# A two-layer product with Mish: x loaded by column quadrants and transposed by VectorE in place of TensorE and DMA transposes

## The chip, the cores and the metric

The kernel runs on one core of a Trainium2 chip. The core has a matrix engine (TensorE, PE in the profile; its weight loads are the row PEld), a vector engine (VectorE, DVE), a scalar engine (ScalarE, ACT), GpSimd (POOL) and SyncE (SP), which here only issues transfers. Transfers (DMAs) are issued from the queues of SP and ACT and carried out by 16 DMA engines. SBUF is the working memory with 128 partitions; PSUM holds the results of the matrix engine in eight banks. The metric is the device time in microseconds; lower is better.

## What is computed

```python
B, S, D, F = 1, 2048, 512, 1792
def reference(x, w1, b1, w2):
    h = jnp.einsum("bsd,df->bsf", x, w1) + b1
    sp = jnp.log1p(jnp.exp(-jnp.abs(h))) + jnp.where(h > 0, h, jnp.zeros_like(h))
    act = h * jnp.tanh(sp)
    return jnp.einsum("bsf,fd->bsd", act, w2)
```

All inputs and the output are bf16. x is 2 MB, w1 and w2 are 1.8 MB each, the output is 2 MB. The activation is Mish.

## The kernel before

The 2048 rows of x are cut into four blocks of 512 rows (16 tiles of 128 rows). For each block a first product makes h transposed: for each of 14 slices f of 128 columns of w1, four matmuls (k = 0 to 3, 128 values of the contraction index each) accumulate in one PSUM bank, 128 x 512; `mish` then reads the bank on ScalarE, adds the bias and writes bf16 to `a_sb` (L159). A second product makes the output tile by tile: for each tile i of 128 rows, 14 matmuls (L198) accumulate over f; VectorE copies the bank to `o_sb` (L204) and SP stores it. Each of the two products has 56 matmuls of 512 columns in a block.

The first product needs x transposed, with the contraction index on the partitions: `xT[:, k, rows]`. Before, this is made in two ways. The first 256 rows are loaded as they lie (`x_nat`, two rows to a partition) and transposed by eight matmuls against an identity (`transpose_x`, L145), four PSUM banks being copied to `xT` by VectorE and ScalarE (L150). The identity is made by GpSimd (L128) and VectorE (L130). All other rows come through four transposing DMAs issued from SP, the first (256 rows) behind a wait for the third filler matmul, the other three behind w2.

Everything is put in order by hand. Each engine has one instruction stream; `Stream.wait` sets a wait on a semaphore and `mark` counts one up. At the start eight filler matmuls on constants (`WARM`, L105) run into bank 7. SP issues, in this order: x_nat; w1 for k = 1, slices 0 to 7; the transposing load of rows 256 to 511; w1 for k = 3; b1; w1 for slices 8 to 13 (768 KB); w2; three transposing loads. ACT issues w1 for k = 0 and k = 2, slices 0 to 7, after the table of Mish is asked for and after b1's buffer is cleared by VectorE. A DMA that waits holds up those behind it on its queue.

The first stage of block 0 opens eight banks at once (`OPEN`, slices 0 to 7) through `first`, with narrow matmuls: tile 0 alone, then tile 1 for k = 0, then tiles 0 and 1, then tiles 2 and 3 together, then the full 512 for k = 3. That makes 8 matmuls of 128 columns, 44 of 256 and 8 of 512; slices 8 to 13 follow with 24 of 512. `spread_b1` turns the bias with four 32x32 transposes on VectorE (L246) and one copy (L248); every `mish` waits for it. In block 0 the second product uses banks 2, 3, 0, 1; in the others banks 0 to 3, while the first product uses banks 4 to 7. The last tile is cut into three parts (`mm2_last`).

Of the kernel before, what the change touches and what calls it, by code (L numbers as in the profile page):

```python
# [5 lines left out]
P = 128  # L6
SQ = 32
WARM = (512,) * 5 + (256,) * 2 + (128,)
# [24 lines left out]
def bass_standalone__dense_activation_mish__prompt_kernel(  # L33
# [17 lines left out]
    w1v = w1.rearrange("(k p) f -> p k f", p=P)  # L51
# [5 lines left out]
    with ExitStack() as es:  # L57
# [3 lines left out]
        x_nat = sb("x_nat", [P, 2, D], BF)  # L61
# [6 lines left out]
        diff = sb("diff", [P, P], dt.int32)  # L68
        ident = sb("ident", [P, P], BF)
# [11 lines left out]
        pool = Stream(nc.gpsimd, sem("c_pool"))  # L81

        def load(q, dst, src, name, transpose=False):
            s = sem(name)
            (q.eng.dma_start_transpose if transpose else q.eng.dma_start)(dst, src).then_inc(s, 16)
            return (s, 16)

        def load_w1(q, ks, a, b):
            return load(q, w1_sb[:, ks, a * P:b * P], w1v[:, ks, a * P:b * P], "s_w1_%d_%d" % (ks.start, a))

        t_w1, t_w2 = {}, {}

        def load_part(q, k0, k1, a, b):
            t = load_w1(q, slice(k0, k1), a, b)
            for f in range(a, b):
                for k in range(k0, k1):
                    t_w1[k, f] = t  # L100

        t_bz = dve.mark(nc.vector.memset(b1_nat[:, :], 0.0))  # L102
        c_w = nc.const_aps.tensor(1.0, [P, P], BF)
        c_m = nc.const_aps.tensor(1.0, [P, 512], BF)
        t_fill = [pe.mark(nc.tensor.matmul(ps[:, 7, 0:n], c_w, c_m[:, 0:n], start=True, stop=True)) for n in WARM]  # L105

        act.eng.preload_act_table(ACT.Mish)  # L107
        act.wait(t_bz)
        for k in (0, 2):
            load_part(act, k, k + 1, 0, OPEN)  # L110
        t_xn = load(sp, x_nat[:, :, :], x2[0:2 * P, :].rearrange("(p j) d -> p j d", p=P), "s_xn")
        load_part(sp, 1, 2, 0, OPEN)
        sp.wait(t_fill[2])
        t_x23 = load(sp, xT[:, :, 2 * P:4 * P], x2[2 * P:4 * P, :], "s_x23", True)
        load_part(sp, 3, 4, 0, OPEN)
# [6 lines left out]
        t_xT = [None]  # L122
        for s in range(1, len(BLOCKS)):
            lo, hi = starts[s], starts[s + 1]
            t_xT.append(load(sp, xT[:, :, lo:hi], x2[lo:hi, :], "s_xT%d" % s, True))


        t_diff = pool.mark(pool.eng.iota(diff[:, :], pattern=[[1, P]], base=0, channel_multiplier=-1))  # L128
        dve.wait(t_diff)
        t_id = dve.mark(nc.vector.tensor_scalar(ident[:, :], diff[:, :], 0, None, ALU.is_equal))  # L130

        free = [[] for _ in range(8)]
        t_cp = {(j, k): t_x23 for j in (2, 3) for k in range(KT)}
        t_mish = {}

        def transpose_x():

            pe.wait(t_xn, t_id)
            for bank, (eng, js, ks) in enumerate(((dve, (0,), (0,)), (act, (1,), (0,)), (dve, (0, 1), (1,)),
                                                  (act, (0, 1), (2, 3)))):  # L140
                n, m = len(ks), len(js)
                for i, k in enumerate(ks):
                    for h, j in enumerate(js):
                        lo = (i * m + h) * P
                        mm = nc.tensor.matmul(ps[:, bank, lo:lo + P], x_nat[:, j, k * P:(k + 1) * P], ident[:, :],  # L145
                                              start=True, stop=True)
                eng.wait(pe.mark(mm))
# [3 lines left out]
                for k in ks:  # L151
                    for j in js:
                        t_cp[j, k] = t
# [107 lines left out]
        for i in range(N0):  # L261
            mm2(i, 0, D, (i + 2) % 4)
# [37 lines left out]
```

## Time and profile before

| | us |
|---|---|
| median of 3 runs | 104.71 |
| the three runs | 104.32, 104.71, 105.37 |
| span of the profiled execution | 103.96 |
| TensorE busy in it | 101.4 |
| ScalarE busy | 39.5 |
| VectorE busy | 13.2 |

The span is the time from the first to the last instruction of one profiled execution, a little less than the device time. "Busy" for matmuls counts overlapped, pipelined instructions, so a busy TensorE is not one at its peak; how fast it runs is read from the distance between the starts of equal matmuls. The chain of waits is followed back from the last instruction, and its pieces are given as start, length and engine with line. In the timeline a row is start, length, engine, line, operation, and how many equal instructions were merged (x). "SPq" and "ACTq" are the queues' issues of DMAs.

### The profile page before, as it was taken

The numbers are of one execution on the slowest core, as the hardware profiler recorded it, in microseconds if no ns is written. First come the engines' busy times: TensorE is split into PE (matmuls) and PEld (weight loads), VectorE is DVE, ScalarE is ACT, GpSimd is POOL, SyncE is SP. The second block draws the span as 40 slices with busy tenths as digits, with TensorE's granted clock in tenths as the row PEclk, the third lists the DMA queues.
The fourth block names the chain that finished last, engine by engine and source line by source line (L and its number), as shares of the span: only waits on it lengthen the run. The fifth ranks groups of instructions, "written<-read, shape, count | busy, mean of one in ns | idle before, by whom it ended". The sixth has DMA issues, their size and how long they took to land.

```text
span 104.0 us, 1180 instructions
## 1 busy us (share of the span) xinstructions
PE 101.4 (98%) x520; PEld 50.0 (48%) x520; DVE 13.2 (13%) x26; ACT 39.5 (38%) x60; POOL 0.4 (0%) x5
## 2 busy tenths in 40 slices
PE   7999999999999999999999999999999999999993
PEld 2888444444444444444444444444444444444472
DVE  1212000112220000022220000022112000021241
ACT  4300899300027777200007777500005777700000
POOL 1000000000000000000000000000000000000000
PEclk9999999999999999999999999999999999999999
DMA  2999999991101000010111000001111000001111
GB/s 70 367 295 368 359 223 193 199 204 50 50 3 47 0 0 6 0 50 12 39 50 50 0 0 3 0 6 50 50 50 50 0 0 0 0 0 56 52 50 50
DMA packets 12833, 7.94 MB, mean 76 GB/s; under 512 B 7836, under 2 KB 12188, under 8 KB 12828
## 3 DMA queue, kind: packets, MB, share of 16 engines
q1 hardware_dynamic: 12396, 7.33, 26.8%
q10 hardware_dynamic: 432, 0.54, 1.5%
q8 instruction: 4, 0.07, 0.3%
q14 instruction: 1, 0.01, 0.0%
HBM read 3.94 MB, written 2.10 MB: 58 GB/s over the span
## 4 chain that ended last, share of the span: by engine, by line
PE 98%; ACT 0%; issue 0%
PE ps L176 47%; PE ps L198 47%; PE ps L105 3%; PE ps L145 1%; ACT o_sb L228 0%
## 5 line engine op out<-in xcount | busy, mean ns | idle before, releaser
L159 ACT ACTIVATE a_sb<-ps,b_sb 128x512 bf16<-128x512 f32 x56 | 37.1, 698 | 48.5 <-PE ps L176 48.5
L176 PE MATMUL ps<-xT,w_sb 128*128 128x512 bf16 (+2 forms) x252 | 50.0, 361 | 0.0
L198 PE MATMUL ps<-w_sb,a_sb 128*128 128x512 bf16 (+3 forms) x252 | 49.1, 355 | 0.0
L176 PEld LDWEIGHTS ps<-xT,w_sb 128*128 128x128 bf16 x252 | 25.0, 101 | 24.1
L198 PEld LDWEIGHTS ps<-w_sb,a_sb 128*128 128x128 bf16 x252 | 23.2, 98 | 25.6
L204 DVE CAST o_sb<-ps 128x512 bf16<-128x512 f32 x15 | 10.4, 692 | 80.8 <-PE ps L198 80.8
L228 ACT ACTIVATE o_sb<-ps 128x64 bf16<-128x64 f32 x1 | 0.2, 224 | 11.5 <-PE ps L198 11.5
L105 PE MATMUL ps<-const-bfloat16-1.0 128*128 128x512 bf16 (+2 forms) x8 | 2.8, 532 | 0.8 <-PEq L285 0.8
L105 PEld LDWEIGHTS ps<-const-bfloat16-1.0 128*128 128x128 bf16 x8 | 1.0, 136 | 2.2 <-issue 2.1
L150 ACT ACTIVATE xT<-ps 128x128 bf16<-128x128 f32 (+1 forms) x2 | 0.9, 438 | 2.2 <-PE ps L145 2.2
L107 ACT ACT_TABLE_LOAD x1 | 1.3, 1283 | 0.7 <-PEq L285 0.7
L246 DVE STREAM_TRANSPOSE b_T<-b_nat 32x32 bf16<-32x32 bf16 x4 | 0.8, 202 | 3.1 <-DMA b_nat<-in_b_dram 3.0
L145 PE MATMUL ps<-ident,x_nat 128*128 128x128 bf16 x8 | 1.0, 309 | 0.0
L150 DVE CAST xT<-ps 128x128 bf16<-128x128 f32 (+1 forms) x2 | 0.7, 358 | 2.5 <-PE ps L145 2.4
L228 DVE CAST o_sb<-ps 128x320 bf16<-128x320 f32 (+1 forms) x2 | 0.8, 392 | 1.5 <-PE ps L198 1.5
L145 PEld LDWEIGHTS ps<-ident,x_nat 128*128 128x128 bf16 x8 | 0.8, 138 | 0.2 <-DMA x_nat<-in_x_dram 0.2
L130 DVE TENSOR_SCALAR ident<-diff 128x128 bf16<-128x128 int32 x1 | 0.2, 227 | 0.2 <-POOL diff L128 0.2
L128 POOL IOTA diff<- 128x128 int32 x1 | 0.2, 234 | 0.4 <-POOLq L285 0.4
L102 DVE MEMSET b_nat<- 32x64 uint32 x1 | 0.1, 112 | 0.8 <-PEq L285 0.8
L248 DVE CAST b_sb<-b_T 128x14 f32<-128x14 bf16 x1 | 0.2, 176 | 0.0
L285 POOL MEMSET const-bfloat16-1.0<- 128x1 bf16 x1 | 0.1, 101 | 0.0
L285 POOL MEMSET const-uint8-127<- 128x1 uint8 x1 | 0.1, 101 | 0.0
(2 smaller groups left out, 0.2 us busy)
## 6 DMA issues: line engine op xcount, KB each, us to landing
out_dram<-o_sb SPq DMA_DIRECT2D x15, 128.0 KB, 1.7
w_sb<-in_w_dram SPq DMA_DIRECT2D x1, 1792.0 KB, 10.5
w_sb<-in_w_dram SPq DMA_DIRECT2D x1, 768.0 KB, 5.8
w_sb<-in_w_dram ACTq DMA_DIRECT2D x2, 256.0 KB, 3.7
w_sb<-in_w_dram SPq DMA_DIRECT2D x2, 256.0 KB, 3.6
x_nat<-in_x_dram SPq DMA_DIRECT2D x1, 256.0 KB, 2.6
out_dram<-o_sb SPq DMA_DIRECT2D x1, 112.0 KB, 1.7
xT<-in_x_dram SPq DMA_TRANSPOSE x4, 5.2
```

The costliest lines, as they stand in the source:

```text
L105: t_fill = [pe.mark(nc.tensor.matmul(ps[:, 7, 0:n], c_w, c_m[:, 0:n], start=True, stop=True)) for n in WARM]
L107: act.eng.preload_act_table(ACT.Mish)
L128: t_diff = pool.mark(pool.eng.iota(diff[:, :], pattern=[[1, P]], base=0, channel_multiplier=-1))
L130: t_id = dve.mark(nc.vector.tensor_scalar(ident[:, :], diff[:, :], 0, None, ALU.is_equal))
L145: mm = nc.tensor.matmul(ps[:, bank, lo:lo + P], x_nat[:, j, k * P:(k + 1) * P], ident[:, :], start=True, stop=True)
L150: t = eng.mark(nc.vector.tensor_copy(dst, src) if eng is dve else act.eng.activation(dst, src, ACT.Copy))
L159: t = act.mark(act.eng.activation(a_sb[:, f, starts[s]:starts[s + 1]], ps[:, bank, 0:n], ACT.Mish, bias=b1_sb[:, f:f + 1]))
L176: return nc.tensor.matmul(ps[:, bank, lo:hi], w1_sb[:, k, f * P:(f + 1) * P], xT[:, k, starts[s] + lo:starts[s] + hi], start=first, stop=( ...
L198: return nc.tensor.matmul(ps[:, bank, 0:hi - lo], a_sb[:, f, i * P:(i + 1) * P], w2_sb[:, f, lo:hi], start=(f == 0), stop=(f == FT - 1))
L204: t = dve.mark(nc.vector.tensor_copy(o_sb[:, i, lo:hi], ps[:, bank, 0:hi - lo]))
L228: t = eng.mark(nc.vector.tensor_copy(dst, src) if eng is dve else act.eng.activation(dst, src, ACT.Copy))
L246: t = dve.mark(nc.vector.transpose(b1_T[j * SQ:(j + 1) * SQ, :], b1_nat[:, j * SQ:(j + 1) * SQ]))
```

## The change

All of x is now loaded in 256-byte pieces. For each of four column quadrants q (128 of the 512 columns) one DMA brings rows lo to hi to the 32 partitions 32q to 32q + 31 of `x_q`, with row 32j + t of x on partition 32q + t. VectorE then transposes 32x32 blocks, with every fourth column of a quadrant taken together, straight into `xT`. So contraction index 4p + k stands on partition p of `xT[:, k]`, and w1 is read with the same numbering. The matmul transposes, the identity, the transposing DMAs, the GpSimd pattern and the interleaved rows of the first 256 outputs are gone. The filler is five matmuls of 512 and two of 128 columns.

Loads of block 0 come in three lots (tile 0, tile 1, tiles 2 and 3), quadrants 0 and 1 on SP and 2 and 3 on ACT, with w1 in pieces of four slices between them; the rest of x comes on SP behind w2, one DMA for each quadrant, 384 KB. On VectorE the transposes of block 0 stand ahead of the bias; those of block 1 stand behind the first output copy, those of blocks 2 and 3 behind the four output copies of block 0. The first stage now runs tile 0 for slices 0 to 3, tile 1 for slices 0 to 3, tiles 0 and 1 for slices 4 to 7, tiles 2 and 3 slice by slice with the Mish after each, and then slices 8 to 13.

```diff
-WARM = (512,) * 5 + (256,) * 2 + (128,)
+WARM = (512,) * 5 + (128,) * 2
-    w1v = w1.rearrange("(k p) f -> p k f", p=P)
+    w1v = w1.rearrange("(p k) f -> p k f", k=KT)
-        x_nat = sb("x_nat", [P, 2, D], BF)
+        x_q = sb("x_q", [P, S // SQ, P], BF)
+        def load_x(eng, q, lo, hi):
+            src = x2[lo:hi, q * P:(q + 1) * P].rearrange("(j t) c -> t j c", t=SQ)
+            t_x[q, lo] = load(eng, x_q[q * SQ:(q + 1) * SQ, lo // SQ:hi // SQ, :], src, "s_x_%d_%d" % (q, lo))
...
+        load_x(sp, 0, 0, P)
+        load_x(sp, 1, 0, P)
+        load_w1(sp, 0, 1, 0, 4)
+        load_w1(sp, 2, 3, 0, 4)
+        load_x(sp, 0, P, 2 * P)
+        load_x(sp, 1, P, 2 * P)
+        load_w1(sp, 0, 2, 4, OPEN)
+        load_x(sp, 0, 2 * P, 4 * P)
+        load_x(sp, 1, 2 * P, 4 * P)
+
+        load_x(act, 2, 0, P)
+        load_x(act, 3, 0, P)
+        load_w1(act, 1, 2, 0, 4)
         act.eng.preload_act_table(ACT.Mish)
+        load_w1(act, 3, 4, 0, 4)
+        load_x(act, 2, P, 2 * P)
+        load_x(act, 3, P, 2 * P)
+        load_w1(act, 2, 4, 4, OPEN)
+        load_x(act, 2, 2 * P, 4 * P)
+        load_x(act, 3, 2 * P, 4 * P)
         sp.wait(t_bz)
         t_b1 = load(sp, b1_nat[0:FT, :], b1.rearrange("(j p) -> j p", p=P), "s_b1")
-        load_part(sp, 0, KT, OPEN, FT)
+        load_w1(sp, 0, KT, OPEN, FT)
         t = load(sp, w2_sb[:, :, :], w2v, "s_w2")
...
+        for q in range(Q):
+            load_x(sp, q, 4 * P, S)
...
+        def spread_x(lo, hi):
+            frm = max(b for b in (0, P, 2 * P, 4 * P) if b <= lo)
+            dve.wait(*[t_x[q, frm] for q in range(Q)])
+            src = x_q[:, lo // SQ:hi // SQ, :].rearrange("p j (r k) -> p k j r", k=KT)
+            for k in range(KT):
+                dst = xT[:, k, lo:hi].rearrange("p (j t) -> p j t", t=SQ)
+                t = dve.mark(nc.vector.transpose(dst, src[:, k]))
+                for i in range(lo // P, hi // P):
+                    t_xT[i, k] = t
...
-        transpose_x()
+        spread_x(0, P)
+        spread_x(P, 2 * P)
+        spread_x(2 * P, 4 * P)
         t_b1c = spread_b1()
-        first(range(4), (0,), (0,))
-        first(range(4), (1,), (0,))
-        first(range(4, OPEN), (0, 1), (0,))
-        first(range(OPEN), (0, 1), (1, 2))
-        first(range(OPEN), (2, 3), (0, 1, 2))
-        first(range(OPEN), None, (3,), True)
+        first(range(4), (0,))
+        first(range(4), (1,))
+        first(range(4, OPEN), (0, 1))
+        for f in range(OPEN):
+            mm1(0, f, (4 + f) % 8, (2, 3))
         for f in range(OPEN, FT):
             mm1(0, f, (4 + f) % 8)
         for i in range(N0):
             mm2(i, 0, D, (i + 2) % 4)
+            if i == 0:
+                spread_x(starts[1], starts[2])
+        for s in range(2, len(BLOCKS)):
+            spread_x(starts[s], starts[s + 1])
```

More of the change, by code (lines that the diff above doesn't have):

```diff
@@ L134, in bass_standalone__dense_activation_mish__prompt_kernel @@
[L134 to L147, printed above, removed]
-                dst = xT[:, ks[0]:ks[0] + n, js[0] * P:(js[-1] + 1) * P]
-                src = ps[:, bank, 0:n * m * P].rearrange("p (k t) -> p k t", k=n)
-                t = eng.mark(nc.vector.tensor_copy(dst, src) if eng is dve else act.eng.activation(dst, src, ACT.Copy))
-                for k in ks:
-                    for j in js:
-                        t_cp[j, k] = t
-                free[bank] = [t]
+        for q in range(Q):
+            load_x(sp, q, 4 * P, S)
@@ L166, in mm1_step @@
             n = BLOCKS[s]
[L167 removed]
+            js = range(n // P) if js is None else js
+            lo, hi = js[0] * P, (js[-1] + 1) * P
             first = k == 0 and lo == 0
```

71 lines of the change are left out of this document (22 added, 49 removed).

## The prediction

> **What bounds the kernel now.** I read the busy table first, then the chain of waits in order of time, then the timeline of the first microseconds.
>
> ```profile
> span 104.0 us, 1180 instructions
> PE 101.4 (98%) x520; PEld 50.0 (48%) x520; DVE 13.2 (13%) x26; ACT 39.5 (38%) x60; POOL 0.4 (0%) x5
> ...
> PEclk9999999999999999999999999999999999999999
> ```
> ```profile
> 0.73 0.04 issue
> 0.77 2.82 PE ps L105 x8
> 3.60 0.85 PE ps L145 x8
> 4.45 13.01 PE ps L176 x84
> 17.46 12.09 PE ps L198 x56
> 29.55 12.09 PE ps L176 x56
> ...
> 102.15 0.02 issue
> 102.18 0.22 ACT o_sb L228
> ```
>
> The chain is TensorE from 0.77 to 102.15 without a hole: eight filler matmuls (L105), eight transposing matmuls (L145), then the real work. Nothing else ends last until the final copy and store. So the change can only act by when the real work starts, by how fast the array runs then, by the number of matmuls, or by opening a hole. How fast it runs shows in the starts of equal matmuls (first and last start, by line and window):
>
> ```profile
> L145 PE MATMUL ps<-ident,x_nat x8: 296/311/311, 3.4 to 4.1; 128*128 128x128 bf16 x8
> L176 PE MATMUL ps<-xT,w_sb x8: 311/311/311, 4.2 to 5.0; 128*128 128x128 bf16 x8
> L176 PE MATMUL ps<-xT,w_sb x38: 272/273/273, 6.1 to 10.2; 128*128 128x256 bf16 x38
> L198 PE MATMUL ps<-w_sb,a_sb x12: 219/219/219, 100.8 to 101.5; 128*128 128x128 bf16 x12
> ```
>
> A 128-wide matmul takes 0.107 us early (0.85 / 8 in the chain) and about 0.056 late (12 between 100.8 and 101.5); the 38 of 256 take 0.11 each; a 512-wide one 0.216 (12.09 / 56). So TensorE runs at half speed from 0.77 to about 6.1 and at full speed after. The page's clock row reads full throughout; the spacing is the better witness. This halves the worth of any earlier start.
>
> ```profile
> 0.74 0.40 SPq L85 DMA_DIRECT2D x_nat<-in_x_dram  x1
> 0.95 0.86 ACTq L85 DMA_DIRECT2D w_sb<-in_w_dram  x2
> 1.20 0.41 SPq L85 DMA_DIRECT2D w_sb<-in_w_dram  x1
> 3.40 0.78 PEld L145 LDWEIGHTS ps<-ident,x_nat 128*128 128x128 bf16 x8 [0.18 <-DMA x_nat<-in_x_dram]
> 4.25 13.22 PE L176 MATMUL ps<-xT,w_sb 128*128 128x128 bf16 x84
> 4.72 0.95 SPq L85 DMA_DIRECT2D w_sb<-in_w_dram  x2
> 7.48 0.90 DVE L246 STREAM_TRANSPOSE b_T<-b_nat 32x32 bf16<-32x32 bf16 x4 [3.00 <-DMA b_nat<-in_b_dram]
> 10.88 7.63 ACT L159 ACTIVATE a_sb<-ps,b_sb 128x512 bf16<-128x512 f32 x13 [5.79 <-PE ps L176]
> ```
>
> x is there at 3.40, the first real matmul starts at 4.25, right behind the eight transposes.
>
> **The change, part by part.** *Fillers and transposes.* The filler is now five of 512 and two of 128: at half speed 5 x 0.427 (4 x 0.107) + 2 x 0.107 from 0.77 ends at 3.12. The eight transposes (0.85) leave the path, with their four PSUM copies on VectorE and ScalarE, the index pattern on GpSimd and the identity. What replaces them is a wait.
>
> *When tile 0 and its weights are there.* The prices:
>
> ```profile
> x_nat<-in_x_dram SPq DMA_DIRECT2D x1, 256.0 KB, 2.6
> w_sb<-in_w_dram ACTq DMA_DIRECT2D x2, 256.0 KB, 3.7
> w_sb<-in_w_dram SPq DMA_DIRECT2D x1, 768.0 KB, 5.8
> w_sb<-in_w_dram SPq DMA_DIRECT2D x1, 1792.0 KB, 10.5
> ```
> ```profile
> 2.50:3.50 1.00, 1.00 (x7) 0.47 (x5) 0.00 (x0) 0.00 (x0) 0.00 (x0) 1.00 1.05 373
> 19.00:20.00 1.00, 1.00 (x6) 0.48 (x5) 0.00 (x0) 0.08 (x1) 0.00 (x0) 1.00 1.27 289
> ```
>
> An issue takes 0.46 of its queue (0.74 to 1.20 on SP). The transfers run at 373 GB/s with weight rows (first window) and at 289 GB/s with the transposing loads (second), whose pieces of x are the nearest row for the new 256-byte pieces. The 256 KB of x_nat landed 2.6 after issue; at 373 GB/s its data need 0.7, so 1.9 is delay at both ends for a first transfer. Tile 0 comes in four quadrants, two on each queue, issued at 0.74 and 1.20: the second pair lands at 1.20 + 1.9 + 0.2 at the latest, 3.3; if only part of the 1.9 repeats, 2.9. w1's first piece (k = 0, 128 KB) is third on SP, issued at 1.65. Counted in bytes (131 KB of x, then 262 KB for k = 0 and 1, 1.05 at 373) it lands at 0.74 + 1.9 + 1.05 = 3.7; counted from its own issue with the full 1.9 and 0.35 of data, 3.9. I take 3.8 for the first real matmul, with 3.3 and 4.25 as ends. VectorE's part is in front of that:
>
> ```profile
> L246 DVE STREAM_TRANSPOSE b_T<-b_nat 32x32 bf16<-32x32 bf16 x4 | 0.8, 202 | 3.1 <-DMA b_nat<-in_b_dram 3.0
> L204 DVE CAST o_sb<-ps 128x512 bf16<-128x512 f32 x15 | 10.4, 692 | 80.8 <-PE ps L198 80.8
> L150 DVE CAST xT<-ps 128x128 bf16<-128x128 f32 x1 | 0.3, 292 | 2.4 <-PE ps L145 2.4
> ```
>
> A transpose of 32 columns takes 0.20 and a column about 1.04 ns (692 - 292 over 384), so 0.30 for 128 columns, 0.43 for 256, 0.70 for 512. The stride of four elements in the source appears in no row: 0.20 and twice the estimate are the ends, I take the estimate. Tile 0's k = 0 is ready by 3.3 to 3.6, under the weights, and each further k 0.30 later, while TensorE spends 0.43 on the four matmuls of a k.
>
> Weighed against this, the Trainium skill, "SBUF — State Buffer", Door 1, says that a transfer into 32 partitions reaches only 8 of 16 ports and measured 189 GB/s at 1 MiB; by that tile 0's bytes would take about 0.25 longer (an estimate), the start would move to 4.05 and the time by half of it, 0.13. No row here shows a 32-partition load, so the sum keeps 289.
>
> *Worth of the start.* By 6.1 the kernel before has done (6.1 - 4.25) / 2 = 0.93 us of full-speed work; a start at 3.8 has done 1.15. Gain 0.22 (ends: 0.48 and 0).
>
> *More matmuls.* The first stage has 32 of 128, 48 of 256 and 24 of 512 where it had 8, 44 and 32: 20 more for the same columns. Four of 0.056 against one of 0.216 cost 0.008, two of 0.109 cost 0.002: in all 0.05.
>
> *The loads that follow.* The same byte count gives: w1 for k = 2, 3 at 4.4 (needed 4.7); x tile 1 at 4.9 and 5.2 transposed (needed 3.8 + 16 x 0.107 = 5.5); w1 for f 4 to 7 at 6.3 (needed 6.7); x tiles 2 and 3 at 7.2, their k = 0 to 3 transposed at 7.6 to 8.9 (needed 8.4 to 8.8); w1 for f 8 to 13 at 9.3 (needed 11.9); w2, 10.5 from an issue inside 4.72 to 5.67 before and now 0.6 later (twelfth on SP, 0.74 + 11 x 0.46 = 5.8), by 16.3 (needed 17.1). Only tiles 2 and 3 touch, for 0.1 at most: 0 to 0.2 is the bound, I take 0. SP now issues nine loads ahead of b1 and w1's last part, which is in those times; ACT issues nine without its wait for the cleared b1, and its table load follows the third.
>
> *The bias and Mish.* On VectorE the bias now stands behind the transposes of tiles 2 and 3: 8.9 + 1.1 (7.48 to the copy's end) = 10.0; the first Mish waits for it from 8.9. Fourteen Mish at 0.57 (7.63 for 13) end at 18.1; the second product needs the last at 17.1 + 13 x 0.216 = 19.9. Hidden.
>
> *The rest of x.*
>
> ```profile
> 20.52 0.69 DVE L204 CAST o_sb<-ps 128x512 bf16<-128x512 f32 x1 [11.93 <-PE ps L198]
> ```
>
> Four loads, 1.57 MB of 256-byte pieces behind w2: 5.4 at 289 GB/s, landing at about 21 to 22. VectorE reaches their transposes after the first output copy (near 20.5), needs 4 x 0.70, and holds back the next three copies, whose banks nobody needs before the next second product near 41. The first matmul that needs them is near 29.3. Cover: 5 us; without it TensorE would stand by the excess.
>
> **Sum.** -0.22 + 0.05 = -0.17 on a span of 103.96. The median shown, 104.71, stands 0.75 above that span, and the runs spread from 104.32 to 105.37. Forecast 104.5, no change that a measurement can tell (about 1%, 1.05 us, is that bound).
>
> **Rivals.**
> *The clock rises late (slower).* Before, TensorE was busy without a break from 0.77, and full speed came after 5.3 us of it. Now it stands from 3.12 to about 3.8. If this pause makes the count begin again, full speed comes at 3.8 + 5.3 = 9.1 and the work until then loses (9.1 - 6.1) / 2 = 1.5: 106.0. Between 0 and 0.7 us lies the length from which it decides; the trace has no pause to show where. For it: full speed needed long activity. Against: the pause is an eighth of those 5.3 us (0.68 / 5.3). The Trainium skill, "TensorE: Matmul & The Clock Gate", Part 1, gives a free-running window of about 3.4 us that must be busy; by it a missed window costs about 1.7, an estimate. The 5.3 us before agree with up to two such windows. Chance 0.25.
> *The start does not move.* If the weights for k = 0 land at 4.2, as with the two 256 KB loads before (3.7 from issues after 0.95), only the 0.05 is left: 104.8. For it: x's small pieces stand ahead of them on both queues. Against: half the bytes. Chance 0.10.
> *The rest of x is late.* At under 120 GB/s the 1.57 MB take over 13 us and the first product of the second block waits from 29.3; at 100 GB/s by some 3 us: 107.5. Against: 289 GB/s in the trace. Chance 0.03.
> *Everything lands at once.* Work starts at 3.3, and the clock rises as before: 104.71 - 0.48 + 0.05 = 104.3. Chance 0.07.
>
> **How the numbers follow.** The forecast has 0.55; its own range is 104.0 to 105.1. Slower by over 1% (above 105.76): most of the late clock (0.19, since a late start of the full speed falls differently in each run) and the late x, 0.03, and 0.02 of scatter: 0.24. Faster by over 1% (below 103.66) needs the early start and a lucky spread of runs: 0.08. Within: 0.68. The range 103.9 to 106.0 leaves out about 0.1 on each side.
>
> **What would show it.** Chain of waits: no L145, a hole or a wait before the first real matmul between 3.1 and 4.0; 104 matmuls in the first stage, then 12.09 per 56 as before. Starts of 128-wide matmuls going from 0.107 to 0.056 apart near 6.1 (right) or near 9 (late clock). Waits of VectorE on x: tile 0 landed by 3.3; the rest by 22. I am wrong if TensorE shows holes after 5 us, if a 128-column transpose takes over 0.45, or if x's loads run well under 289 GB/s.

## The result and the profile after

| | before | after |
|---|---|---|
| median, us (six runs each) | 104.84 | 109.67 |
| lowest to highest, us | 104.32 to 105.37 | 109.29 to 110.30 |
| span of the profiled execution, us | 103.96 | 108.98 |
| end of the last matmul in it, us | 102.15 | 107.18 |

The ratio of after to before is 1.046, with a 95% interval of 1.0415 to 1.0508: the change costs 4.6%, where no measurable change was forecast. The matmuls end 5.03 us later, and the tail behind them is the same, so the loss is in the array's own row. Here and below, a run more than 1.5% above the fastest of its kernel counts in the medians and not in the ratios. The page of the kernel after:

```profile
span 109.0 us, 1232 instructions
...
PE 103.2 (95%) x522; PEld 51.8 (48%) x531; DVE 22.5 (21%) x47; ACT 38.9 (36%) x58; POOL 0.2 (0%) x4
...
GB/s 43 237 237 238 357 347 218 142 169 147 39 48 48 48 0 6 0 0 48 23 25 48 48 3 0 6 0 48 48 29 19 48 0 0 0 6 48 48 48 48
```

TensorE's share fell from 98% to 95%, and one slice of the GB/s row is 2.72 us: from 2.7 to 10.9 us the loads ran at 237 GB/s. The chain of waits of the kernel after (start, length, what; L173 is the first product, L192 the second; "issue" is time in which nothing that the profile shows was waited for):

```profile
3.53 6.24 DMA w_sb<-in_w_dram
9.77 0.05 issue
9.81 4.46 PE ps L173 x20
...
14.36 3.01 ACT a_sb L160 x5
17.36 5.13 PE ps L173 x23
22.49 5.61 PE ps L192 x26
```

Before, the chain was TensorE from 0.77 on. Now it runs through a load of weights from 3.53 to 9.77, and TensorE's unbroken part begins at 9.81. (From 14.36 to 17.36 the chain follows the Mish; the matmuls start 0.11 apart there, as before and after it, but for 0.32 at 17.04, which leaves room for two matmuls missing from the trace.) The timeline shows what came before:

```profile
0.77 2.50 PE L103 MATMUL ps<-const-bfloat16-1.0 128*128 128x512 bf16 x7 [0.77 <-PEq L274]
...
3.58 0.89 DVE L146 STREAM_TRANSPOSE xT<-x_q 128x128 bf16<-128x128 bf16 x4 [2.67 <-DMA x_q<-in_x_dram]
...
4.92 1.89 PE L173 MATMUL ps<-xT,w_sb 128*128 128x128 bf16 x16 [1.65 <-DMA w_sb<-in_w_dram]
...
7.28 0.89 DVE L146 STREAM_TRANSPOSE xT<-x_q 128x128 bf16<-128x128 bf16 x4 [2.81 <-DMA x_q<-in_x_dram]
...
7.65 1.89 PE L173 MATMUL ps<-xT,w_sb 128*128 128x128 bf16 x16 [0.84 <-DVE xT L146]
...
9.81 10.52 PE L173 MATMUL ps<-xT,w_sb 128*128 128x256 bf16 x61 [0.28 <-DMA w_sb<-in_w_dram]
...
11.66 1.42 DVE L146 STREAM_TRANSPOSE xT<-x_q 128x256 bf16<-128x256 bf16 x4 [3.50 <-DMA x_q<-in_x_dram]
```

Three waits stand where before there was none: for the first weights until 4.92, for tile 1 of x until 7.65, and for w1's slices 4 to 7 until 9.81. The matmuls' durations, by start, show the array's speed. The same view as in the prediction, for two stretches of the kernel after:

```profile
L173 PE MATMUL ps<-xT,w_sb x20: 394/421/422, 9.8 to 13.8; 128*128 128x256 bf16 x20
L173 PE MATMUL ps<-xT,w_sb x28: 272/273/310, 14.1 to 17.0; 128*128 128x256 bf16 x28
```

A 256-wide matmul is recorded with 421 ns and starts 0.21 after the last one until 14.1, then with 273 ns and 0.11: full speed came at 14.1, against 6.1 before. That accounts for the whole loss:

- The first matmul of the product starts 4.92 − 4.25 = 0.67 later. Sixteen of 128 at half speed take 16 × 0.107 = 1.71, so the first lot is issued by 6.63 and TensorE stands 1.02 until 7.65; the second lot is issued by 9.36, and it stands 0.45 until 9.81. Together 2.14.
- From 4.92 to 14.12, less these 1.47 of standing, 7.73 us of real work ran at half speed, which loses 3.87. Before it was (6.10 − 4.25) / 2 = 0.93. The difference is 2.94.
- 2.14 + 2.94 = 5.08, against 5.03 measured.

The loads in the two stretches, before and then after (the last column is GB/s, the one before it the share of the 16 DMA engines that were busy, which this view can show above 1):

```profile
2.60:6.00 3.40, 3.40 (x26) 2.63 (x24) 0.72 (x2) 0.88 (x2) 0.00 (x0) 1.00 1.11 355
6.00:10.40 4.40, 4.40 (x42) 3.93 (x41) 0.98 (x5) 0.00 (x0) 0.00 (x0) 1.00 1.03 334
```
```profile
2.60:6.00 3.40, 1.75 (x15) 1.23 (x13) 0.89 (x4) 0.83 (x1) 0.00 (x0) 1.00 0.79 212
6.00:10.40 4.40, 3.28 (x27) 2.60 (x26) 0.89 (x4) 0.00 (x0) 0.00 (x0) 1.00 1.02 243
```

In the second stretch the 16 DMA engines are as busy as before (share 1.02 against 1.03) and move 27% less (243 against 334).

### The profile page after: what moved, and what is told of

Same layout as the page of the kernel before. It is cut to its first block, busy times and chain, and to the rows that moved or that the text cites. A ratio compares the mean times of both kernels' runs of the same rounds, so it can differ in the third digit from the quotient of the medians.

```text
span 109.0 us, 1232 instructions
## 1 busy us (share of the span) xinstructions
PE 103.2 (95%) x522; PEld 51.8 (48%) x531; DVE 22.5 (21%) x47; ACT 38.9 (36%) x58; POOL 0.2 (0%) x4
## 4 chain that ended last, share of the span: by engine, by line
PE 86%; DMA 6%; ACT 3%; SPq 2%; issue 1%; ACTq 0%
PE ps L192 44%; PE ps L173 42%; DMA w_sb<-in_w_dram 6%; ACT a_sb L160 3%; SPq L83 2%; ACT o_sb L222 0%; ACTq L26 0%
## 5 line engine op out<-in xcount | busy, mean ns | idle before, releaser
L173 PE MATMUL ps<-xT,w_sb 128*128 128x512 bf16 (+2 forms) x268 | 53.0, 364 | 3.0 <-DMA w_sb<-in_w_dram 1.9
L192 PE MATMUL ps<-w_sb,a_sb 128*128 128x512 bf16 (+3 forms) x247 | 48.8, 355 | 0.3
L173 PEld LDWEIGHTS ps<-xT,w_sb 128*128 128x128 bf16 x272 | 27.7, 107 | 27.5 <-DMA w_sb<-in_w_dram 2.5
L192 PEld LDWEIGHTS ps<-w_sb,a_sb 128*128 128x128 bf16 x252 | 23.2, 98 | 25.6
L146 DVE STREAM_TRANSPOSE xT<-x_q 128x512 bf16<-128x512 bf16 (+2 forms) x24 | 10.5, 500 | 10.5 <-DMA x_q<-in_x_dram 10.5
L222 ACT ACTIVATE o_sb<-ps 128x64 bf16<-128x64 f32 x1 | 0.2, 223 | 11.5 <-PE ps L192 11.5
L103 PE MATMUL ps<-const-bfloat16-1.0 128*128 128x512 bf16 (+1 forms) x7 | 2.5, 534 | 0.8 <-PEq L274 0.8
## 6 DMA issues: line engine op xcount, KB each, us to landing
x_q<-in_x_dram SPq DMA_DIRECT2D x4, 384.0 KB, 10.5
```

Of the source, the lines that this page charges most:

```text
L146: t = dve.mark(nc.vector.transpose(dst, src[:, k]))
L173: return nc.tensor.matmul(ps[:, bank, lo:hi], w1_sb[:, k, f * P:(f + 1) * P], xT[:, k, starts[s] + lo:starts[s] + hi], start=first, stop=( ...
L192: return nc.tensor.matmul(ps[:, bank, 0:hi - lo], a_sb[:, f, i * P:(i + 1) * P], w2_sb[:, f, lo:hi], start=(f == 0), stop=(f == FT - 1))
L222: t = eng.mark(nc.vector.tensor_copy(dst, src) if eng is dve else act.eng.activation(dst, src, ACT.Copy))
```

## The experiments

Two causes were possible after this reading, and they feed each other: loads that come late, and a clock that rises late because of the holes. A first group tells them apart; a second changes the loads in the changed kernel; a third puts the new parts into the old order. The times are medians; each ratio is to the kernel before, run beside it on the same chip. In the runs with another order of x or of w1's rows, what is multiplied is not the reference's.

| run | what | us | ratio (95%) |
|---|---|---|---|
| e8_pause | before, fewer fillers | 105.96 | 1.011 (1.007 to 1.015) |
| e1_fill | after, fillers in the holes | 109.03 | 1.041 (1.036 to 1.047) |
| e5_w1rows | after, w1 rows as before | 109.79 | 1.043 (1.037 to 1.049) |
| e6_w1wide | after, w1 in wider pieces | 109.95 | 1.047 (1.042 to 1.052) |
| e2_ports | after, x to 128 partitions | 107.98 | 1.031 (1.025 to 1.037) |
| e3_rows1k | after, x in pieces of 1024 bytes | 109.29 | 1.037 (1.025 to 1.049) |
| e4_one | after, x in one load a lot, 128 partitions, 1024 bytes | 108.36 | 1.033 (1.025 to 1.041) |
| e12_one256 | as e4, 256 bytes | 109.59 | 1.048 (1.042 to 1.053) |
| e7_all | e4, e5 and e6 together | 108.31 | 1.027 (1.019 to 1.034) |
| e9_all_fill | e7 with a longer filler | 106.33 | 1.015 (1.010 to 1.020) |
| e10_ports_fill | e2 with fillers | 108.36 | 1.033 (1.029 to 1.038) |
| e11_old_order | old order and plain loads, VectorE transposes | 105.02 | 1.002 (0.999 to 1.004) |
| e13_x_alone | old order, x in quadrants | 108.36 | 1.030 (1.024 to 1.036) |
| e14_q128 | e13, 128 partitions | 107.98 | 1.026 (1.018 to 1.035) |
| e15_r32 | e13, 1024 bytes | 107.95 | 1.024 (1.016 to 1.032) |
| e16_one | e13, one load a lot, 128 partitions, 1024 bytes | 105.65 | 1.006 (1.003 to 1.010) |
| e17_one256 | as e16, 256 bytes | 108.11 | 1.031 (1.026 to 1.036) |

### The clock, and the loads

**e8_pause.** The kernel before, with three fillers in place of eight, so that TensorE stands before its transposes and nothing else is late.

```diff
-WARM = (512,) * 5 + (256,) * 2 + (128,)
+WARM = (512,) * 3
```

> The kernel before with only three filler matmuls (they end near 2.05), so that TensorE stands until x is there at 3.4; nothing else is changed, the first real matmul starts at 4.25 as before. Theory 'late clock': the pause of 1.3 us makes full speed come between 6.8 and 10.2 instead of 4.2 to 7.6, on the mean 2.6 later, half of it lost: time 105.3 to 106.4 against 104.6. Rival 'the clock does not mind': 104.4 to 104.9.

The same view of the first product's matmuls in e8_pause, for two stretches:

```profile
L176 PE MATMUL ps<-xT,w_sb x16: 314/421/421, 4.9 to 8.0; 128*128 128x256 bf16 x15, 128*128 128x128 bf16 x1
L176 PE MATMUL ps<-xT,w_sb x28: 272/273/310, 8.2 to 11.2; 128*128 128x256 bf16 x28
```

A pause of 1.3 us moved full speed from 6.1 to 8.3, and (8.3 − 6.1) / 2 is 1.1; the median rose by 1.0. So a late clock by itself exists, at half of its lateness, as the first rival had it.

**e1_fill.** The changed kernel with fillers in its three holes, so that the clock can rise while the loads stay as they are.

```diff
-WARM = (512,) * 5 + (128,) * 2
+WARM = (512,) * 9 + (128,) * 2
...
+        def fill(n):
+            for _ in range(n):
+                pe.mark(nc.tensor.matmul(ps[:, 3, 0:512], c_w, c_m[:, 0:512], start=True, stop=True))
...
         first(range(4), (0,))
+        fill(4)
         first(range(4), (1,))
+        fill(2)
```

> The changed kernel with TensorE kept busy in its three early holes by matmuls on constants (four of 512 columns more at the start, four between tile 0 and tile 1, two before slices 4 to 7). The loads are untouched. Theory 'late loads': the holes and the half speed both come from data that arrive late, and full speed alone buys little, because tiles 2 and 3 still land at 11.5 us and their transposes end near 13.1: full speed by 6 to 7.5 us, first stage done about 1 us earlier, time 108.4 to 109.0 against 109.67. Rival 'late clock': the 2.9 us lost to half speed are the main cost by themselves: time 106.5 to 107.2.

The timeline of e1_fill (L236 is the filler in the holes):

```profile
7.28 1.05 PE L173 MATMUL ps<-xT,w_sb 128*128 128x128 bf16 x16
...
8.17 0.60 PE L236 MATMUL ps<-const-bfloat16-1.0 128*128 128x512 bf16 x2
...
9.34 1.92 PE L173 MATMUL ps<-xT,w_sb 128*128 128x256 bf16 x16 [0.57 <-DMA w_sb<-in_w_dram]
...
11.01 1.10 DVE L146 STREAM_TRANSPOSE xT<-x_q 128x256 bf16<-128x256 bf16 x3 [3.23 <-DMA x_q<-in_x_dram]
...
11.52 0.61 PE L173 MATMUL ps<-xT,w_sb 128*128 128x256 bf16 x2 [0.26 <-DVE xT L146]
```

Sixteen matmuls now take 1.05 in place of 1.89: the array is at full speed, and was from 3.6. The time gains half a per cent at most (1.041 against 1.046, with intervals that overlap), because TensorE runs into the same loads sooner: slices 4 to 7 at 9.34, tiles 2 and 3 only at 11.5. With these late loads a quick clock is worth little.

### Which loads, in the changed kernel

**e5_w1rows** numbers w1's rows as before, **e6_w1wide** loads slices 0 to 7 of each k at once, as before, in pieces of 2048 bytes in place of 1024.

```diff
-    w1v = w1.rearrange("(p k) f -> p k f", k=KT)
+    w1v = w1.rearrange("(k p) f -> p k f", p=P)
```

> The changed kernel with w1's rows numbered as before (row k * 128 + p on partition p instead of 4p + k); x stays 4p + k, so what is multiplied is not the reference's. Pieces, bytes and order are the same. Theory 'interleaved rows' (every fourth row of w1 is slow to read: single pieces of w1 took 0.4 to 0.9 us in the changed kernel): the weights of slices 4 to 7 land before 8.8 instead of 9.77 and 10.35, long pieces vanish, time 108.5 or less. Rival 'small pieces of x': no change, 109.3 to 110.0.

```diff
-        load_w1(sp, 0, 1, 0, 4)
-        load_w1(sp, 2, 3, 0, 4)
+        load_w1(sp, 0, 1, 0, OPEN)
+        load_w1(sp, 2, 3, 0, OPEN)
...
-        load_w1(sp, 0, 2, 4, OPEN)
...
```

> The changed kernel with w1's slices 0 to 7 in four loads of 256 KB (2048-byte pieces, one for each k, as before) instead of four of 128 KB and two of 256 KB in 1024-byte pieces. The order of the rest stays. Theory 'small pieces of w1': the bytes up to tiles 2 and 3 are the same, and they land by 10.3 instead of 11.54; the first matmul is later by up to 0.5 since k = 0 brings twice the bytes; time 109.0 or less. Rival: the small pieces of x alone set the rate, tiles 2 and 3 land at 11.3 or later, time 109.3 to 110.3.

Neither moved the time beyond its interval, so the form of w1 alone does not make the loss. Its narrower pieces do have a part in the low rate: in e6 the two stretches ran at 278 and 312 GB/s, against 212 and 243, and tiles 2 and 3 landed at 9.44 in place of 11.54. What that gained went to the first matmul, which waited until 5.74 for a load of twice the size. In e5 the two stretches ran at 220 and 265.

**e2_ports, e3_rows1k, e4_one** change x's loads: to all 128 partitions, still in four loads of 256-byte pieces; to 32 partitions in pieces of 1024 bytes; and in one load for a lot, 128 partitions, 1024 bytes. x's values then lie in another order.

```diff
+            m, b = (hi - lo) // P, lo // SQ
+            src = x2[lo:hi, q * P:(q + 1) * P].rearrange("(j p) c -> p j c", p=P)
+            t_x[q, lo] = load(eng, x_q[:, b + q * m:b + (q + 1) * m, :], src, "s_x_%d_%d" % (q, lo))
```

> The changed kernel with x's loads writing all 128 partitions instead of 32: the same number of DMAs, the same 256-byte pieces of the same bytes in the same order, 128 partitions x fewer pieces each. x lies in another arrangement in SBUF, so what is multiplied is not the reference's. Theory 'partitions' (a load into 32 partitions is slow in itself): the rest of x runs at 250 GB/s or more and lands by 25 instead of 27.65, tile 1 lands before 6.2 instead of 7.16, time 107.5 or less. Theory 'pieces' (256-byte pieces) and theory 'count' (many small DMAs): no change, 109.3 to 110.0.

```diff
+            n = (hi - lo) // Q
+            src = x2[lo + q * n:lo + (q + 1) * n, :].rearrange("(n t) d -> t n d", t=SQ)
+            dst = x_q[q * SQ:(q + 1) * SQ, lo // SQ:hi // SQ, :].rearrange("t (n j) c -> t n (j c)", j=Q)
+            t_x[q, lo] = load(eng, dst, src, "s_x_%d_%d" % (q, lo))
```

> The changed kernel with x's loads in 1024-byte pieces (whole rows): the same number of DMAs, still 32 partitions each, the same bytes in all, a quarter of the pieces. x lies in another arrangement in SBUF, so what is multiplied is not the reference's. Theory 'pieces': the early loads and the rest of x gain a rate of 300 GB/s or more, tile 1 lands before 6.2, time 107.5 or less. Theory 'partitions': 32 partitions still bind, no change, 109.3 to 110.0. Theory 'count': the same, no change.

```diff
+            src = x2[lo:hi, :].rearrange("(n p) d -> p n d", p=P)
+            dst = x_q[:, lo // SQ:hi // SQ, :].rearrange("p (n j) c -> p n (j c)", j=Q)
+            t = load(eng, dst, src, "s_x_%d" % lo)
...
-        load_x(sp, 1, 0, P)
...
```

> The changed kernel with one DMA for each lot of x (tile 0 on SP, tile 1 and tiles 2 and 3 on ACT, the rest on SP) in place of four, 128 partitions and 1024-byte pieces. x lies in another arrangement in SBUF, so what is multiplied is not the reference's. All three theories of the loads expect a gain here: tile 1 landed by 5.5, no hole over 0.3 us after the first real matmul, time 104.5 to 106.5. If it stays above 108, the loads of x are not the cause, and the weights' pieces or their row order are. Theory 'count' expects this run alone to gain, the two others near 109.7.

Tiles 2 and 3 landed at 9.71 in e2, 10.42 in e3 and 8.49 in e4, against 11.54, and full speed came at 8.2, 10.5 and 10.1. Each brings the loads forward, none gains half of the loss, and e3's gain is within its interval. The times of e2 and e4 lie in none of the windows that were expected, e3's at the edge of "no change". By what was expected of e4, a time above 108 would clear x's loads; e13 and e16, below, show that this reading would have been wrong: the late clock and w1's narrower pieces were still in it.

**e12_one256** is e4 in pieces of 256 bytes.

```diff
-            src = x2[lo:hi, :].rearrange("(n p) d -> p n d", p=P)
+            src = x2[lo:hi, :].rearrange("(p n) (j c) -> p (n j) c", p=P, j=Q)
...
```

> The run with one DMA for each lot of x (e4_one), but in 256-byte pieces (each quarter row goes to a place of its own with a gap; 128 partitions; four times the pieces). What is multiplied is not the reference's. Against e4_one only the pieces differ; against e2_ports (four DMAs for each lot, 256-byte pieces, 128 partitions) the number of DMAs does. Theory 'count': as in e4_one, all of the first 1.57 MB landed by 8.9 (8.49 there), time 107.7 to 108.8. Theory 'pieces': landed at 9.4 or later, near e2_ports' 9.71.

Tiles 2 and 3 landed at 10.61 in place of e4's 8.49, and what e4 had gained is gone: in one load to 128 partitions the small pieces cost by themselves. The number of loads is not idle either: e2 has the same small pieces and 128 partitions, in four loads over both queues, and is faster than e12 (1.031 against 1.048). Why is not shown.

**e7_all** takes e4, e5 and e6 together; **e9_all_fill** is e7 with ten fillers of 512; **e10_ports_fill** is e2 with e1's fillers before tile 0 and between tiles 0 and 1.

> The changed kernel with all three at once: one DMA for each lot of x (128 partitions, 1024-byte pieces), w1's rows as before, w1's slices 0 to 7 in 2048-byte pieces; VectorE still transposes, the filler stays short. What is multiplied is not the reference's. Theory 'late loads, then late clock': the loads keep 340 GB/s or more from 3 to 9 us, tiles 2 and 3 land by 7.8, only the pause before the first matmul and one before tile 1 are left; time 105.5 to 107.0. If the clock played no part, it would come to 104.6 to 105.4. If it stays above 107.5, something else in the change costs.

```diff
-WARM = (512,) * 5 + (128,) * 2
+WARM = (512,) * 10 + (128,) * 2
```

> The run with one DMA for each lot of x, w1's rows and pieces as before (e7_all), and five filler matmuls of 512 columns more, which end near 5.2, where its first real matmul started (5.1). What is multiplied is not the reference's. Theory 'late loads and late clock together are the whole loss': with neither, the first product of block 0 ends at about 18.1 against 17.3 before (the first matmul is still 0.9 later), time 105.0 to 106.0, some 2.5 under e7_all's 108.31. Rival 'something else in the change costs' (the transposes' order, narrow matmuls, the Mish behind them): it stays above 107.

```diff
-WARM = (512,) * 5 + (128,) * 2
+WARM = (512,) * 9 + (128,) * 2
...
         first(range(4), (0,))
+        fill(4)
```

> The run with x's 256-byte pieces written to 128 partitions (e2_ports) and filler matmuls through its two pauses (four of 512 more at the start, four between tile 0 and tile 1). What is multiplied is not the reference's. Loads as in e2_ports: tile 1 at 6.8, slices 4 to 7 at 8.9, tiles 2 and 3 at 9.7. Theory 'loads bind once the clock is up': tiles 2 and 3 are ready from 10.1 to 11.2, the first product of block 0 ends near 19 to 19.5, time 106.3 to 107.0. If the clock alone were left: 105.0 to 105.8.

The loads of e7 and e9 run at the old rate and more: the stretches 2.6 to 6.0 and 6.0 to 10.4 of e7_all:

```profile
2.60:6.00 3.40, 1.56 (x12) 0.92 (x9) 0.89 (x4) 0.00 (x0) 0.00 (x0) 1.00 1.04 381
6.00:10.40 4.40, 4.29 (x34) 3.70 (x33) 3.18 (x13) 0.00 (x0) 0.00 (x0) 1.00 1.07 372
```

Yet e7 is still 2.7% slower, with full speed only at 11.0; e9, where it comes at 4.8, is 1.5% slower. e7 missed its expectation by 1.3 us, e9 by 0.3. Loads alone take the ratio from 1.046 to 1.027, the clock alone (e1) to 1.041, both to 1.015. That is more than the sum, as if each hid the other, but the intervals are too wide to show the excess. What is left in e9 is in its first stage: the weights for k = 0, second on SP, land at 5.38, so that the first matmul starts at 5.43 in place of 4.25, and those for k = 2 land at 6.34, with TensorE standing until 6.38. e10 missed its expectation by over 1 us, and its fillers gained nothing over e2 (1.033 against 1.031). Its loads of x and w1 are those of e2, but in the profiled execution tiles 2 and 3 landed at 10.67 in place of 9.71 and slices 4 to 7 up to 0.8 later, and TensorE stood 1.20 for the slices: equal loads can differ by about 1 us from one execution to another, and a profile of one execution can't settle differences of that size.

### One part at a time, in the old order

**e11_old_order** keeps the order of the kernel before, its w1 and its bank order, but loads x in plain rows and makes all transposes on VectorE; e11b_old_order is a second execution of it with its own profile. x's columns are numbered 4p + k there and w1's rows are not. The filler is longer than before.

```diff
-WARM = (512,) * 5 + (256,) * 2 + (128,)
+WARM = (512,) * 5 + (256,) * 5 + (128,) * 2
...
-        t_x23 = load(sp, xT[:, :, 2 * P:4 * P], x2[2 * P:4 * P, :], "s_x23", True)
+        t_x23 = load(sp, x_r[:, 2:4, :], x2[2 * P:4 * P, :].rearrange("(n p) d -> p n d", p=P), "s_x23")
...
-        transpose_x()
+        spread(x_nat[:, :, :], t_xn, 0, 2 * P)
+        spread(x_r[:, 2:4, :], t_x23, 2 * P, 4 * P)
```

> The kernel before, its order of matmuls and loads kept, with every transpose moved to VectorE's 32x32 blocks (no identity, no transposing matmuls, no transposing DMAs; all of x in plain loads of whole rows into 128 partitions) and the filler lengthened to about 4.2, where the first weights land. VectorE's blocks land in an arrangement of x that is not the reference's, so what is multiplied is not. Theory 'the transposes on VectorE are free, the loss is in how and in which order the loads come': first real matmul at 4.1 to 4.3, no hole over 0.3 after it, 104.4 to 105.2, the same as before within 0.5. Rival 'VectorE's transposes cost by themselves': 105.8 or more, with TensorE waiting for VectorE.

> e11_old_order once more, for a profile: eleven of its twelve runs took 104.5 to 105.4, but the profiled one 275, with every 512-wide matmul at about 0.6 us to the end. Expected: 104.5 to 105.5, first real matmul at 4.1 to 4.3, no hole after it.

The chain of waits of e11b_old_order (L157 is the first product):

```profile
2.24 4.48 DMA x_r<-in_x_dram
...
6.74 0.46 DVE xT L136
...
7.24 9.70 PE ps L157 x56
16.94 12.09 PE ps L179 x56
```

The ratio is 1.002 (0.999 to 1.004): in place of TensorE's and the transposing DMAs', VectorE's transposes, with the longer filler, cost no time that the runs can tell, and gain none. They are not free on the way: x for tiles 2 and 3 lands at 6.72, VectorE's first transpose of it stands on the chain for 0.46, and TensorE stands 0.5 until 7.24, where no hole over 0.3 was expected. The first product still ends at 16.94, before 17.46 of the kernel before, because in this execution full speed came at 3.5 in place of 6.1, which is worth 0.9. How much of the equal time the filler pays for was not tried apart.

**e13_x_alone** is the kernel before with x loaded and transposed as in the kernel after (four loads a lot, 32 partitions, 256 bytes) and w1's rows numbered to match; w1's pieces, the order of the loads on SP and the order of the matmuls stay; two of the four loads of each lot now go through ACT, the first two of them ahead of w1. The filler runs to 4.6.

```diff
-        t_xn = load(sp, x_nat[:, :, :], x2[0:2 * P, :].rearrange("(p j) d -> p j d", p=P), "s_xn")
+        t_xn = [load_x(eng, q, 0, 2 * P) for q, eng in enumerate((sp, sp, act, act))]
...
-        t_x23 = load(sp, xT[:, :, 2 * P:4 * P], x2[2 * P:4 * P, :], "s_x23", True)
+        t_x23 = [load_x(eng, q, 2 * P, 4 * P) for q, eng in enumerate((sp, sp, act, act))]
```

> The kernel before's order of matmuls, w1's slices 0 to 7 in 2048-byte pieces one k after the other, filler to about 4.6; x comes as in the changed kernel, in column quadrants of 32 partitions and 256-byte pieces (tiles 0 and 1 in one lot), w1's rows as 4p + k, transposes on VectorE. It computes the reference. Against e11_old_order (105.02, the same as before) only x's loads and w1's row numbers differ. Theory 'x's quadrant loads are the cause': first weights later than 5.0, tiles 2 and 3 later than 9, holes after the first matmul, 107 or more. Theory 'w1's narrow pieces and the order that needs four k at once are': 105.0 to 106.0. Between the two if both count.

The chain of waits of e13_x_alone:

```profile
1.71 4.33 DMA w_sb<-in_w_dram
6.05 0.05 issue
6.09 13.93 PE ps L159 x84
20.02 12.09 PE ps L181 x56
```

x itself is early (its first lot landed by 3.6), and what is late is the weights behind it: k = 0 at 6.05 in place of 4.1, and the product starts 1.84 later than before. Part of that is place in the queue: k = 0 is issued at 1.71 where it was 0.95, and k = 1 lands ahead of it, at 5.34. Full speed, which came at 6.1 before, comes at 9.4; with (9.4 − 6.1) / 2 = 1.7 us lost to half speed, against 0.93, the clock adds 0.75. The first product ends at 20.02, 2.56 later, which is the sum of the two. After its start there is no hole, where holes were expected. x's loads, with the late clock that they bring, carry 3.0 of the 4.6% in this order.

**e14_q128, e15_r32, e16_one, e17_one256** take e13's loads of x apart, as e2, e3, e4 and e12 did in the changed kernel; the lines of their loads are those of these four.

> e13_x_alone with one thing changed: each of the four loads of x in a lot goes to all 128 partitions, still in 256-byte pieces (another order of rows and columns, so the output is not the reference's). In e13 the weights for k = 0 landed at 6.05 us and the run took 108.36. Theory 'the 32 partitions': 104.8 to 106.4, weights for k = 0 landed by 4.9. Theory 'the 256-byte pieces': 107.0 or more, weights at 5.5 or later. Theory 'four loads instead of one': also 107.0 or more.

> e13_x_alone with one thing changed: each of the four loads of x in a lot brings whole rows of 1024 bytes, still to 32 partitions (the output is not the reference's). Theory 'the 32 partitions': 107.0 or more, weights for k = 0 landed at 5.5 us or later. Theory 'the 256-byte pieces': 104.8 to 106.4, weights by 4.9. Theory 'four loads instead of one': 107.0 or more.

> e13_x_alone with x in one load for each lot, whole rows of 1024 bytes to all 128 partitions (the output is not the reference's); weights, their numbering, order and filler as in e13. If the form of x's loads is the cause: 104.4 to 105.7, weights for k = 0 landed by 4.4 us, ratio under 1.01. If the numbering of w1's rows or the longer filler carries part of e13's 3%: 106.0 or more.

> e16_one with one thing changed: each load of x (one for a lot, 128 partitions) is cut into pieces of 256 bytes instead of 1024 (the output is not the reference's). In e16 the first lot landed at 4.75 us and the first matmul of the product started at 5.37; 105.65. Theory 'only the count of loads matters (four for a lot instead of one)': 105.2 to 106.2, first lot landed by 5.0. Theory 'the 256-byte pieces cost by themselves too': 106.8 or more, first lot landed at 5.4 or later.

The weights for k = 0 landed at 5.88 in e14 and 6.78 in e15, and the product started near 5.9 and 6.8. The chains of waits of e16_one and, after it, e17_one256:

```profile
0.73 4.02 DMA x_q<-in_x_dram
...
4.78 0.46 DVE xT L139
5.23 0.14 issue
5.37 5.58 PE ps L160 x52
```
```profile
0.73 4.96 DMA x_q<-in_x_dram
...
5.71 0.46 DVE xT L138
6.17 0.14 issue
6.30 13.98 PE ps L159 x84
```

In e16 the first lot took 4.02 us from its issue, in pieces of 256 bytes 4.96. With all three departures from plain rows (quadrants) the ratio is 1.030; without the 32 partitions 1.026; without the small pieces 1.024; with the small pieces alone 1.031; with none 1.006. These ratios do not rank the departures, for the clock differs among them. In the profiled executions the product of e14 and of e15 ran at full speed from its start, e13's at half speed until 9.4, and e17's at half speed from 7.2 to 10.6 (the last section), which lost e13 and e17 1.7 us each. Of the 2.5 us between e16 and e17, 0.93 is the later start and most of the rest this stretch at half speed. e17 also differs from e16 in the cut of the rows and in a gap behind each piece in `x_q`.

The rest of x, which comes behind w2 when little else is moved, shows the forms without the clock. The columns are windows of the profile and the GB/s in them:

| run | partitions | piece, bytes | loads for a lot | window, us | GB/s |
|---|---|---|---|---|---|
| e16_one | 128 | 1024 | one | 15.2 to 17.8 | 349 |
| e15_r32 | 32 | 1024 | four | 17.7 to 19.7, 20.0 to 21.5 | 231, 223 |
| e14_q128 | 128 | 256 | four | 16.7 to 18.6, 18.0 to 19.5 | 224, 216 |
| e17_one256 | 128 | 256 | one | 17.5 to 18.8, 19.0 to 21.4 | 164, 236 |
| e13_x_alone | 32 | 256 | four | 17.4 to 19.2, 19.3 to 21.0 | 203, 141 |

Small pieces alone take about a third off the rate or more, 32 partitions in four loads of whole rows about a third, and both together two fifths or more. So each departure costs, and that the ratios do not add up is no sign that one of them alone is the cause. With small pieces, four loads or one made no clear difference here (e14, e17); for e15 the partitions or the number of loads were not tried apart. e16's 0.6%, where e11 has none, goes with x and weights landing together at 4.6 to 4.8 instead of x at 3.3; e16 also has another numbering of w1, another cut of the rows and a longer filler, and these were not told apart. The threshold of e16's expectation for the weights (4.4) was missed by 0.2, its time and ratio were met.

The Trainium skill, "DMA: Bandwidth & Descriptors", Why small descriptors are slow, gives a fixed cost for each packet, 3 of 11 cycles or 27% for 256 bytes from HBM. The first lot agrees in size: 4.96 against 4.02 is 23% more, fixed delays included. The rest of x does not: 216 to 224 GB/s in e14 against 349 in e16 is over half as long again. That e15 is as slow with pieces of 1024 bytes is outside that rule.

## Why the prediction was wrong

**The step that failed** is "The loads that follow": it counted bytes at 373 GB/s for weights and 289 for x (for tile 0, ahead of k = 0, at 373 too). In the prediction's terms and in the trace (landings, us):

| | forecast | landed |
|---|---|---|
| x, tile 0 | 2.9 to 3.3 | 3.5 |
| w1, k = 0, slices 0 to 3 | 3.8 | 4.87 |
| w1, k = 2 and 3, slices 0 to 3 | 4.4 | 5.58 and 5.94 |
| x, tile 1 | 4.9 | 7.16 |
| w1, slices 4 to 7 | 6.3 | 9.77 and 10.35 |
| x, tiles 2 and 3 | 7.2 | 11.54 |
| w1, slices 8 to 13 | 9.3 | 13.45 |
| w2 | 16.3 | 19.48 |
| the rest of x | 21 to 22 | 27.65 |

Two choices in it were wrong. The row of the transposing loads was taken as nearest to the new 256-byte pieces, and it is another kind of transfer; the measured rate of the whole mix, with w1's pieces narrower too, is 212 to 243 GB/s, and of x's quadrants behind w2 it is 147 and 170 (19.7 to 22.0 and 22.2 to 24.4). And the cost was thought of as x's own, while the weights behind x came late, as e13 shows: there x is early and the weights late. The margins at these steps were stated as 0.3 to 0.4 us (4.9 and 5.2 against 5.5, 6.3 against 6.7), so rates lower by 27% (243 against 334) and 40% (212 against 355) were enough to open holes; the text had the bound 0 to 0.2 for the touch at tiles 2 and 3 where the doubtful rate should have been carried through all of these loads. The page's list of the issues of DMAs shows it (size, us from issue to landing):

```profile
x_q<-in_x_dram SPq DMA_DIRECT2D x4, 384.0 KB, 10.5
...
w_sb<-in_w_dram SPq DMA_DIRECT2D x2, 128.0 KB, 3.4
w_sb<-in_w_dram ACTq DMA_DIRECT2D x2, 128.0 KB, 3.6
w_sb<-in_w_dram SPq DMA_DIRECT2D x1, 256.0 KB, 6.2
```

A load of 256 KB of weights takes 6.2 from issue to landing, where one of the same size took 3.7 before.

**The late clock** had the right mechanism and, for one pause, the right price: e8_pause lost 1.0 us for a full speed 2.2 later, where 1.5 for 3.0 later was worked out. The forecast had one pause, 3.1 to 3.8. In the kernel after there were three, to 4.9, 7.6 and 9.8, and full speed came at 14.1 in place of the rival's 9.1; with the holes filled (e1) it came at 3.6. The rival was worked out with the loads on time; that both come together, one making the other, was in no case, and so the range ended at 106.0.

**The Trainium skill's rule on 32 partitions** ("SBUF — State Buffer", Door 1) was priced at 0.13 us for tile 0 alone. e15 agrees with its direction (32 partitions and whole rows, 1.024 against 1.006, and 231 against 349 GB/s for the rest of x), but has four loads as well; and the price was on the wrong bytes, since tile 0 landed 0.2 late and everything else of the first stage by 1.1 to 4.3.

**What held.** The filler ended and the eight transposes left the path as forecast; tile 0 landed within 0.2 of the later end. VectorE's transposes took 0.27, 0.40 and 0.67 for 128, 256 and 512 columns, against 0.30, 0.43 and 0.70; four of 128 are through in 0.89. The bias and the Mish stayed hidden, and 20 more matmuls cost nothing visible. The rest of x came 6 us later than forecast but was needed only at 34.6, because everything before it was late too; in the old pace its first transposes (28.4) would have been in time for the 29.39 of the kernel before and the last (30.3) about 0.2 late, so the cover of 5 us named for it was in truth used up. The forecast gain, 0.22 for an earlier start, did not come: the first matmul of the product started 0.67 later, at 4.92, outside the stated ends of 3.3 and 4.25. The rival "the start does not move" stopped at 4.25 as well. The distance between the span and the device time, taken as 0.75 from the median, is 1.3 within one run (110.3 against 109.0); that is no part of the error.

## What to carry to other kernels

A load is not only bytes over a rate: in these runs pieces of 256 bytes, or four loads into 32 partitions, moved a third less in the same time, and the weights queued behind them came late. Where the first stage has a margin of a few tenths of a microsecond, the price of a doubtful rate has to be carried through every load behind it and not only through its own. Holes and the clock belong in one case: a hole in the first 10 us can be paid a second time at half speed (e8, e13, e17), though it is not always (e14, e15), and removing either cause alone left most of the loss (e1) or over half of it (e7). VectorE transposes in 32x32 blocks can replace TensorE's and the DMA's at no measurable cost, if x is loaded in whole rows and the filler is lengthened (e11); no version here beat the kernel before.

## What the runs showed of the hardware

**The clock can fall again after a hole of 2 us.** In e17_one256 the last filler matmul starts at 4.14 and ends at about 4.4, and TensorE then stood until 6.3. Its matmuls by start, in three stretches:

```profile
L159 PE MATMUL ps<-xT,w_sb x12: 216/219/289, 6.3 to 7.1; 128*128 128x128 bf16 x8, 128*128 128x256 bf16 x4
L159 PE MATMUL ps<-xT,w_sb x16: 393/418/418, 7.2 to 10.4; 128*128 128x256 bf16 x16
L159 PE MATMUL ps<-xT,w_sb x23: 272/273/297, 10.6 to 13.0; 128*128 128x256 bf16 x23
```

Full speed is kept for 0.9 us after the hole, then 3.4 us run at half speed without any gap, then full speed again. The page's clock row shows it here, as a dip to 8 and 5 in the third and fourth slice, where the other pages that have this row read full throughout:

```profile
PEclk9985999999999999999999999999999999999999
```

The Trainium skill, "TensorE: Matmul & The Clock Gate", Part 1, has a free-running window of 3.4 us: a busy one raises the clock, an idle one lets it fall. The distances agree: the filler reached full speed at 3.8, and 7.2 and 10.6 follow 3.4 apart. The fall does not: the window that lost the clock was not idle but busy for 1.3 to 1.5 of its 3.4 us, about 40%. Full speed came between 2.8 and 5.3 us after the first filler where TensorE was kept busy (3.5 in e11b, 3.6 in e1, 4.8 in e9, 6.1 before, counted from the span's start), so the 5.3 us read off one profile was no fixed need. In the kernel after, counting back from 14.12 in steps of 3.41, the window from 7.29 to 10.70 was busy for 1.71 + 0.89 = 2.60, 76%, and did not raise it. The share alone does not settle it: in e16 full speed came at 5.8, behind a window that was as busy (the filler to 4.56, the product from 5.37).

**A slow array for a whole execution.** One of e11's twelve executions took 275.4 us, which its ratio leaves out; its chain of waits has 56 matmuls of 512 in 33.27 us, 0.59 each in place of 0.216, and its clock read 1.0:

```profile
5.62 33.41 PE ps L157 x84
39.02 33.27 PE ps L179 x56
```
